# A fused attention and feed-forward layer on one core: which feed-forward weights are split when, and seven softmax steps on another engine

## The chip, the cores and the metric

The kernel runs on one core of a Trainium2 chip. A core has a matrix engine (TensorE, "PE" in the profile), a vector engine (VectorE, "DVE"), an activation engine (ScalarE, "ACT"), a general engine (GpSimd, "POOL"), and DMA queues that are fed by SyncE ("SP") and here also by ACT. Each engine runs its own instructions strictly in order and waits on semaphores for the others. The metric is the device time of one execution in microseconds; lower is better. Everything is float32; TensorE multiplies in its "fp32r" type, and the kernel gets its precision from splitting each operand into a high and a low part and adding three products.

## The reference

```python
def _A_ref(x, wqkv, wo):            # 32 heads of 16, window 8, dilation 2
    qkv = (x @ wqkv).reshape(B, S, 3, H, Dh)...
    idx = pos[:, None] - (jnp.arange(8) * 2)[None, :]
    logits = jnp.einsum("bhsd,bhswd->bhsw", q, kg) * Dh ** -0.5
    attn = softmax(where(idx >= 0, logits, -1e9), axis=-1)
    o = jnp.einsum("bhsw,bhswd->bhsd", attn, vg)
    return o... @ wo

def _B_ref(x, w1, b1, w2, b2):
    h = x @ w1 + b1
    r = where(h > 0, h, 0)
    return (r * r) @ w2 + b2

x  = A_x                            # 1 x 2048 x 512, w1 512 x 1792, w2 1792 x 512
xn = layernorm(x)
return x + _A_ref(xn, A_wqkv, A_wo) * silu(_B_ref(xn, B_w1, B_b1, B_w2, B_b2))
```

## The kernel before

**Phase 1** goes over the 2048 rows in 16 tiles of 128 (`a` and `b` are an even and an odd tile of one turn of the loop). Each tile is normalised, brought into the transposed layout and split (`xt`, high and low), and multiplied by the split weights `wq` for q, k and v: `qkv(t, s)`, twelve matmuls of 128x512 into one of four PSUM buffers. ACT copies the result to a staging tile `stg`, and per pair of tiles a DMA on SP stores it to `sq`, `sk` or `sv` in DRAM. From there the attention's loads (`load_u`, on ACT's DMA queue) bring q, k and v back in another layout.

**The attention** goes over eight units of 256 rows (u = 0 to 7) and runs on DVE beside everything else: four products and reductions for the logits (`qk`, tiles `pr` and `L`), the softmax in two parts (`soft_a`: maximum `mx`, subtraction, exponential on ACT; `soft_b`: sum `sm`, reciprocal, multiplication), four products and reductions with v (`av`, tiles `pv` and `v`), and a store to `so`. Unit 0 does its softmax in two halves; the other seven do it whole (`h is None`). The stream is written as a generator that yields an estimated cost ahead of each step, and `pump` emits steps as long as the planned clock of DVE stays near the planned clock of PE. So the numbers that are yielded set where a step stands among DVE's other instructions.

**Phase 2** goes over four chunks of 512 rows (c = 0 to 3) and, in each, over 14 slices of 128 hidden columns (f = 0 to 13): `up(c, f)` (twelve matmuls into `ph`, one of two PSUM buffers), then ACT makes relu and squares (`h`), DVE makes the low part (`lowh(f)`), and `down(c, f - 2)` (twelve matmuls into `pb`). `up(0, 0)` and `up(0, 1)` are already done at the end of phase 1. `out_product` multiplies the attention's output by `wot`; `gate` and `finish` add `b2t`, apply the gate, add the rows of x and store.

**The weights of a slice**, `w12[f]`, are 8 KB a partition: w1's columns and w2's rows, each as high and low part. `load_w` brings in both raw pieces by DMA on SP, `split_w` makes the high parts on ACT (`high`) and the low parts on GpSimd or DVE (`low`). Slices below `NKEEP` (6) live in the pool `keep` and are loaded and split in phase 1; slices 0 and 1 are loaded at the first tiles and their low parts are made on DVE. The later ones live in the pool `p2`, are loaded during chunk 0 and split three slices ahead of their use.

**The pool `p2`** is opened where phase 1's pools (`px`, `pstg`, `pwq`, `pxT`) are closed, in the same memory. The first instruction of each engine that writes into `p2` therefore waits until everything that read or wrote the closed pools is over, the last store of a staging tile among it. That is decided for the pools as a whole, not by address.

Instructions of PE, DVE, ACT and GpSimd stay in the order in which they are written; the DMAs on SP are ordered by the framework's scheduler. All compute instructions carry the line of one helper (L80) in the profile, so tiles tell them apart.

Of the kernel before, what the change touches and what calls it, by code (L numbers as in the profile page):

```python
# [8 lines left out]
F32 = mybir.dt.float32  # L9
FR = mybir.dt.float32r  # L10
# [4 lines left out]
P = 128  # L15
S = 2048
D = 512
F = 1792
KT = D // P
NF = F // P  # L20
HD = 16
W = 8
# [10 lines left out]

PASSES = ((0, 0), (0, 1), (1, 0))

NKEEP = 6

WARM = 18
WARM2 = 3
# [11 lines left out]
def body(ctx: ExitStack, tc: tile.TileContext, x, wqkv, wo, w1, b1, w2, b2, out):  # L51
# [32 lines left out]
    PE, V, A, G = Ordered(nc.tensor, "PE"), Ordered(nc.vector, "V"), Ordered(nc.scalar), Ordered(nc.gpsimd)  # L84
# [4 lines left out]
    dma = nc.sync.dma_start  # L89

    const = ctx.enter_context(tc.tile_pool(name="const", bufs=1))
# [3 lines left out]
    keep = ctx.enter_context(tc.tile_pool(name="keep", bufs=1))  # L95
# [12 lines left out]
    def piece(name):  # L108
        return keep.tile([P, 512], F32, name=name, tag="z", bufs=4)
# [76 lines left out]
                    G.memset(mask[:4 * blk + 4, :n, w], -1e9)  # L186

    b1t = const.tile([P, NF], F32, name="b1t")

    sq = dram.tile([4, S, P], F32, name="sq")  # L190
    sk = dram.tile([4, HALO + S, P], F32, name="sk")
# [32 lines left out]
    def attention():  # L224

        tiles, Ls, landing, exps = {}, {}, {}, set()

        def qk(u, s):  # L230
            i0 = 2 * s
            yield from there("k", u)
            yield from there("q", u)
            q, k, L = tiles["q", u], tiles["k", u], Ls[u]
            yield 2350
            pr = att.tile([P, W, 2 * P], F32, name=f"pr{u}_{s}", tag="pr")
            qv = q[:, i0:i0 + 2, :].rearrange("p i c -> p (i c)")[:, None, :].to_broadcast([P, W, 2 * P])
            kv = k[:, i0:i0 + 2 * W, :].rearrange("p (w i) c -> p w (i c)", i=2)
            V.tensor_mul(pr, kv, qv)
            yield 2300  # L240
            V.tensor_reduce(
                out=L[:, i0 * 8:(i0 + 2) * 8, :].rearrange("p m w -> p w m"),
                in_=pr.rearrange("p w (g d) -> p w g d", d=HD), axis=AX.X, op=OP.add)

        def there(n, u):
            while (n, u) not in tiles:
                yield None
            not_before(landing[n, u])


        def part(u, h):
            n = BI * 8 // 2
            return slice(0, 2 * n) if h is None else slice(h * n, h * n + n)

        def soft_a(u, h=None):
            yield 1500
            m = part(u, h)
            L, n = Ls[u][:, m], m.stop - m.start
            if u == 0:
                i = slice(m.start // 8, m.stop // 8)  # L260
                lm = L.rearrange("p (i h) w -> p i h w", h=8)
                V.tensor_add(lm, lm, mask[:, i, None, :].to_broadcast([P, n // 8, 8, W]))
            mx = att.tile([P, n], F32, name=f"mx{u}_{h}", tag="mx")
            V.tensor_reduce(out=mx, in_=L, axis=AX.X, op=OP.max)
            V.tensor_sub(L, L, mx[:, :, None].to_broadcast([P, n, W]))

            def exp():
                A.activation(L, L, AF.Exp)
                exps.add((u, h))

            defer(clock["V"] + BEHIND, exp)

        def soft_b(u, h=None):
            while (u, h) not in exps:
                yield None
            yield 2100
            m = part(u, h)
            L, n = Ls[u][:, m], m.stop - m.start
            sm = att.tile([P, n], F32, name=f"sm{u}_{h}", tag="sm")
            V.tensor_reduce(out=sm, in_=L, axis=AX.X, op=OP.add)  # L280
            V.reciprocal(sm, sm)
            V.tensor_mul(L, L, sm[:, :, None].to_broadcast([P, n, W]))

        def av(u, s):
            i0 = 2 * s
            yield from there("v", u)
            v, L = tiles["v", u], Ls[u]
            yield 2400

            pr = att.tile([P, W // 2, 2 * P, 2], F32, name=f"pv{u}_{s}", tag="pr")  # L290
            vv = v[:, i0:i0 + 2 * W, :].rearrange("p (a e i) (h d) -> p a e (i h) d", e=2, i=2, d=HD)
            l = L[:, i0 * 8:(i0 + 2) * 8, :].rearrange("p m (a e) -> p a e m", e=2)
            V.tensor_mul(pr.rearrange("p a (g d) e -> p a e g d", d=HD), vv,
                         l[:, :, :, :, None].to_broadcast([P, W // 2, 2, 16, HD]))
            yield 2300
            V.tensor_reduce(
                out=v[:, i0:i0 + 2, :].rearrange("p i c -> p (i c)"), in_=pr.rearrange("p w n e -> p n w e"),
                axis=AX.XY, op=OP.add)

        def store(u):  # L300
            v = tiles.pop(("v", u))
            row = so[0, u * UP:u * UP + 1, :]
            dst = bass.AP(tensor=row.tensor, offset=row.offset, ap=[[BI * P, NB], [S * P, 4], [1, BI * P]])
            dma(dst, v[:, :BI, :].rearrange("p i c -> p (i c)"))
            done_units[0] = u + 1

        def load(u, names):
            if u == NU:
                return
            for n in names:  # L310
                while done_tiles[n][0] < 2 * (u + 1):
                    yield None

                def start(n=n):
                    tiles[n, u] = load_u(n, u)
                    landing[n, u] = clock["PE"] + LOAD

                defer(max(clock["V"] + FREE if u else 0, done_tiles[n][1][u] + LAND), start)

        yield from load(0, "kqv")  # L320

        for u in range(NU + 1):
            if u < NU:
                Ls[u] = att.tile([P, BI * 8, W], F32, name=f"L{u}", tag="L", bufs=2)
                for s in range(4):
                    yield from qk(u, s)
                    if u == 0 and s % 2:
                        yield from soft_a(0, s // 2)
                if u:
                    yield from soft_a(u)  # L330
                yield from load(u + 1, "kq")
                if u == NU - 1:
                    yield from load(u, "v")
            if u == 0:
                yield from soft_b(0, 0)
            for s in range(4):
                if u > 1 or (u == 0 and s < 2) or (u == 1 and s >= 2):
                    yield from av(max(u - 1, 0), s)
            if u == 0:
                yield from soft_b(0, 1)  # L340
            if u:
                store(u - 1)
                if u < NU - 1:
                    yield from load(u, "v")
                if u < NU:
                    yield from soft_b(u)
# [17 lines left out]

    w12 = {}

    def load_w(pool, f):
        w12[f] = pool.tile([P, 2, 2, 512], FR, name=f"w{f}")

        r1, r2 = (p2.tile([P, 512], F32, name=f"{n}{f}", tag="xr", bufs=2) if f in (6, 9) else piece(f"{n}{f}")  # L370
                  for n in ("w1r", "w2r"))
        dma(r1.rearrange("p (k c) -> p k c", c=P), w1[:, f * P:(f + 1) * P].rearrange("(k p) c -> p k c", p=P))
        dma(r2, w2[f * P:(f + 1) * P, :])
        raws[f] = r1, r2

    def split_w(f, eng=G):
        for i, r in enumerate(raws.pop(f)):
            split(w12[f][:, 0, i], w12[f][:, 1, i], r, eng)

# [182 lines left out]
    norm(2)  # L562
    stats(3)
    constants()
    for f in range(2):
        load_w(keep, f)
    qkv(0, 0, lambda: highs(2, 0))
    trans(2)
    lows(2, 0)
# [10 lines left out]
    norm(4)  # L580
    norm(5)
    shuffle(4)
    split_w(0, V)
    pump(LATE)
    qkv(1, 2)
    split_w(1, V)
    pump(LATE)
    for a in range(2, NT, 2):
        b, more = a + 1, a + 2 < NT
        later = a + 4 < NT  # L590

        def weights(f):
            if 2 <= f < NKEEP:
                load_w(keep, f)
            if 2 <= f - 1 < NKEEP:
                split_w(f - 1)

        if later:
# [6 lines left out]
            mean(b + 4)  # L605
        pump(LATE)
        qkv(b, 0)
        weights(a - 5)
        if a + 2 < TURN:
            lowx(a + 2)  # L610
            trans(b + 2)
# [21 lines left out]
        if not more:  # L633
            pump()
            up(0, 1)
            lowh(0)
        weights(b - 5)
        pump(LATE)
        qkv(a, 2)
        pump(LATE)  # L640
        qkv(b, 2)
        if a == NT - 4:
            dma(b1t, b1.rearrange("(f p) -> p f", p=P))
        if a >= TPC:
            for t in (a, b):
                dma(sx[t // TPC][:, t % TPC], xt.pop(t).bitcast(F32))
# [3 lines left out]


    p2 = ctx.enter_context(tc.tile_pool(name="p2", bufs=1))
    pws, gs = {}, {}

    def down(pb, f, j):
# [60 lines left out]
        eng.tensor_add(z[:, cols], z[:, cols], xt[:, cols])  # L716
        dma(tile_rows(out, t)[:, cols], z[:, cols])

    wot = p2.tile([P, 2, 4, 512], FR, name="wot")
    b2t = p2.tile([P, D], F32, name="b2t")  # L720
    dma(b2t, b2[None, :].to_broadcast([P, D]))

    for c in range(NCH):
        last = c == NCH - 1
# [3 lines left out]
        for f in range(2, NF):  # L728
            if c == 0:
                for i in (6, 7) if f == 2 else (f + 5,):  # L730
                    if i < NF:
                        load_w(p2, i)
            up(c, f)
            pump()
            if c == 0 and f == 3:
# [4 lines left out]
                        rows = wo[q * P + 64 * i:q * P + 64 * i + 64, :].rearrange("(g p) n -> p g n", g=2)  # L740
                        dma(rwo[i][32 * q:32 * q + 32], rows)
            if c == 0:
                if NKEEP <= f + 3 < NF:
                    split_w(f + 3)
                if 6 <= f < 10:
                    split(wot[:, 0, f - 6], wot[:, 1, f - 6], rwo[(f - 6) // 2][:, (f - 6) % 2], G)
# [98 lines left out]
```

## Time and profile before

| what | us |
|---|---|
| median of 3 runs | 499.7 (496.83, 500.06, 499.7) |
| the profiled execution's own time | 495.58 |
| its span, first to last instruction | 493.8 |
| PE busy in the span | 487.5 |
| phase 1 up to the last `qkv` matmul | about 146.4 |
| chunk 0, to the start of `up(1, 2)` | about 228.5 |
| end of the last matmul | about 490.1 |

The profiled execution was 4.1 us shorter than the median of the runs, of which no trace exists. In the page's lines a group reads "line engine operation out<-in", then the count, the busy time, the mean of one, and the idle time ahead of it with what ended it. In a timeline the first two columns are the start and the duration in us. PE's busy time covers nearly the whole span; the places where something else sets the pace are short.

### The profile page before, as it was taken

The page shows a single profiled execution, that of the slowest core. Times are in us where ns is not written, and L with a number is a line of the kernel's source. Part 1 is how long each engine was busy: PE and PEld are TensorE (multiplying, and loading weights), DVE is VectorE, ACT ScalarE, POOL GpSimd, SP SyncE. Part 2 cuts the span into 40 slices and gives each one's busy share as a digit, 9 for nine tenths or more (in the row PEclk, how much of TensorE's full clock was granted, in tenths as well). Part 3 has the DMA queues.
Part 4 walks back from the last instruction along what each step waited for, and adds up shares of the span by engine and source line. Part 5 has one row for each costly group of instructions (what it writes and reads, how often), then busy time and mean ns, then how long its engine had stood idle before and what let it go on. Part 6 is the DMA issues. An engine that isn't in the chain of part 4 may idle for free.

```text
span 493.8 us, 5860 instructions
## 1 busy us (share of the span) xinstructions
PE 487.5 (99%) x2154; PEld 401.1 (81%) x2154; DVE 431.7 (87%) x370; ACT 211.0 (43%) x377; POOL 97.9 (20%) x105
## 2 busy tenths in 40 slices
PE   8999999999999999999999999999999999999997
PEld 5888888888888888887888888888888888888886
DVE  5925798998999999998999998899999889999445
ACT  5636455563343665316333324432252354313331
POOL 1311015571000779300112000112100011220000
PEclk9999999999999999999999999999999999999999
DMA  7999979769977892653406408043241805030222
GB/s 287 297 287 341 304 238 313 225 238 323 372 228 262 203 274 65 202 212 118 127 31 216 181 22 329 4 164 123 85 161 43 328 2 202 1 127 1 85 85 86
DMA packets 48520, 88.79 MB, mean 180 GB/s; under 512 B 5372, under 2 KB 32364, under 8 KB 45676
## 3 DMA queue, kind: packets, MB, share of 16 engines
q1 hardware_dynamic: 44172, 54.87, 35.3%
q10 hardware_dynamic: 4320, 33.56, 19.1%
q8 instruction: 17, 0.28, 0.2%
q14 instruction: 11, 0.09, 0.1%
HBM read 57.94 MB, written 27.32 MB: 173 GB/s over the span
## 4 chain that ended last, share of the span: by engine, by line
PE 83%; DVE 9%; issue 4%; ACT 2%; DMA 1%; ACTq 0%; POOL 0%; DVEq 0%; POOLq 0%
PE pq L80 27%; PE ph L80 24%; PE pb L80 24%; PE pw L80 8%; DVE v L80 2%; DVE pr L80 2%; DVE h L80 2%; DVE pv L80 1%; DMA x<-in_A_x 1%; ACT ph L80 0%; DVE sm_None L80 0%; ACT z L80 0%; DVE z L80 0%; ACT h L80 0%; PE pxT L80 0%
## 5 line engine op out<-in xcount | busy, mean ns | idle before, releaser
L80 PE MATMUL pb<-w,h 128*128 128x512 f32 x672 | 160.6, 389 | 0.0
L80 PEld LDWEIGHTS pb<-w,h 128*128 128x128 f32 x672 | 126.1, 188 | 26.2
L80 PE MATMUL ph<-xU,w 128*128 128x512 f32 x504 | 120.7, 389 | 0.3 <-DVE h L80 0.3
L80 PEld LDWEIGHTS ph<-xU,w 128*128 128x128 f32 x504 | 94.6, 188 | 20.2 <-DVE h L80 0.7
L80 ACT ACTIVATE ph<-ph,b1t 128x512 f32<-128x512 f32 x56 | 37.0, 661 | 163.0 <-PE ph L80 158.4
L80 PE MATMUL pq<-wq,xt 128*128 128x512 f32 x432 | 98.7, 390 | 0.0
L80 PEld LDWEIGHTS pq<-wq,xt 128*128 128x128 f32 x432 | 81.0, 188 | 17.2 <-ACT stg L80 0.3
L80 DVE TENSOR_TENSOR pr<-k,q 128x2048 f32<-128x2048 f32 x32 | 75.4, 2356 | 0.3
L80 DVE TENSOR_TENSOR pv<-v,L 128x2048 f32<-128x2048 f32 x32 | 73.8, 2305 | 0.4
L80 DVE TENSOR_REDUCE L<-pr 128x128 f32<-128x2048 f32 x32 | 72.9, 2279 | 0.6
L80 DVE TENSOR_REDUCE v<-pv 128x256 f32<-128x2048 f32 x32 | 72.9, 2279 | 0.6
L80 POOL TENSOR_TENSOR z<-z,xr 128x512 f32<-128x512 f32 x12 | 23.2, 1936 | 214.7 <-DVE z L80 209.9
L80 DVE TENSOR_TENSOR h<-ph,h 128x512 fp32r<-128x512 f32 x56 | 38.3, 683 | 19.9 <-ACT ph L80 19.9
L80 PE MATMUL pw<-wot,oT 128*128 128x512 f32 (+1 forms) x204 | 45.9, 376 | 0.0
L80 PEld LDWEIGHTS pw<-wot,oT 128*128 128x128 f32 x204 | 36.8, 188 | 7.1
L80 PE MATMUL ph<-xT,w 128*128 128x512 f32 x168 | 40.7, 391 | 0.0
L80 ACT ACTIVATE stg<-pq 128x512 f32<-128x512 f32 x48 | 27.2, 595 | 26.4 <-PE pq L80 16.9
L80 PEld LDWEIGHTS ph<-xT,w 128*128 128x128 f32 x168 | 31.5, 188 | 7.0 <-DVE h L80 0.4
L80 ACT ACTIVATE h<-ph 128x512 fp32r<-128x512 f32 x56 | 33.7, 601 | 1.8
L80 ACT ACTIVATE ph<-ph 128x512 f32<-128x512 f32 x56 | 33.3, 595 | 0.0
L80 PE MATMUL pq<-wq,xT 128*128 128x512 f32 x132 | 31.7, 398 | 0.0
L80 POOL TENSOR_TENSOR w<-w1r,w 128x512 fp32r<-128x512 f32 x12 | 18.9, 1577 | 57.1 <-DMA rwo<-in_A_wo 48.8
(66 smaller groups left out, 309.9 us busy)
## 6 DMA issues: line engine op xcount, KB each, us to landing
k<-sk ACTq DMA_DIRECT2D x8, 1408.0 KB, 8.1
v<-sv ACTq DMA_DIRECT2D x8, 1408.0 KB, 8.3
sx<-xt SPq DMA_DIRECT2D x12, 512.0 KB, 5.5
xU<-sx ACTq DMA_DIRECT2D x6, 1024.0 KB, 5.4
x<-in_A_x SPq DMA_DIRECT2D x16, 256.0 KB, 5.0
sk<-stg SPq DMA_DIRECT2D x8, 512.0 KB, 7.1
sq<-stg SPq DMA_DIRECT2D x8, 512.0 KB, 5.6
q<-sq ACTq DMA_DIRECT2D x8, 512.0 KB, 8.4
```

Source lines behind the costliest of these rows:

```text
L80: return tc.keep_in_program_order(f(*a, **k))
```

## The change

`NKEEP` goes from 6 to 3. Slices 0, 1 and 2 are loaded and split in phase 1, one per turn of the loop and later than before, all on GpSimd. Slices 3 and 4 are loaded in the turn before the last and split right after phase 1's pools are closed, into `p2`; slice 5 is loaded there, and split after `up(0, 2)`. From slice 6 on the split follows `up(0, f)` three slices ahead, as before. `b2t` moves from `p2` into the pool `const` and is loaded in phase 1. `w12[f]` is now allocated at the split and no longer at the load. In the softmax of units 1 to 7 the subtraction of the maximum and the multiplication by the reciprocal sum go from DVE to GpSimd, and the yielded costs go from 1500 to 700 and from 2100 to 1400.

```diff
-NKEEP = 6
+NKEEP = 3
...
+    b2t = const.tile([P, D], F32, name="b2t")
...
-            yield 1500
+            yield 1500 if h is not None else 700
...
-            V.tensor_sub(L, L, mx[:, :, None].to_broadcast([P, n, W]))
+            (G if h is None else V).tensor_sub(L, L, mx[:, :, None].to_broadcast([P, n, W]))
...
-            yield 2100
+            yield 2100 if h is not None else 1400
...
-            V.tensor_mul(L, L, sm[:, :, None].to_broadcast([P, n, W]))
+            (G if h is None else V).tensor_mul(L, L, sm[:, :, None].to_broadcast([P, n, W]))
...
-    def load_w(pool, f):
-        w12[f] = pool.tile([P, 2, 2, 512], FR, name=f"w{f}")
+    def load_w(f):
...
     def split_w(f, eng=G):
+        w12[f] = (keep if f < NKEEP else p2).tile([P, 2, 2, 512], FR, name=f"w{f}")
...
-    for f in range(2):
-        load_w(keep, f)
...
-    split_w(0, V)
...
-    split_w(1, V)
...
-            if 2 <= f < NKEEP:
-                load_w(keep, f)
-            if 2 <= f - 1 < NKEEP:
+            if 0 <= f < NKEEP:
+                load_w(f)
+            if 0 <= f - 1 < NKEEP:
                 split_w(f - 1)
...
-        weights(a - 5)
+        weights(a // 2 - 2)
...
-        weights(b - 5)
...
         if a == NT - 4:
             dma(b1t, b1.rearrange("(f p) -> p f", p=P))
+            dma(b2t, b2[None, :].to_broadcast([P, D]))
+            for f in (NKEEP, NKEEP + 1):
+                load_w(f)
...
     p2 = ctx.enter_context(tc.tile_pool(name="p2", bufs=1))
+    for f in (NKEEP, NKEEP + 1):
+        split_w(f)
+    load_w(NKEEP + 2)
+    wot = p2.tile([P, 2, 4, 512], FR, name="wot")
...
-                if NKEEP <= f + 3 < NF:
+                if f + 3 < NF:
                     split_w(f + 3)
```

Three places show what this does to the engines' queues. The number behind a name is the framework's; `w3`, `ph0_2`, `L2` and so on are slice 3, `up(0, 2)`, unit 2. What stands in brackets are the semaphores that an instruction waits for; DMAHW0 to 7 tell of the landing of DMAs.

ACT's queue at the end of phase 1, before: from the last copy of a `qkv` result (tile 15, v) on.

```order
L80 ACTIVATE stg14_2_1401<-pq15_2_1408 128x4x128 [waits PE_49]
L80 DMA k3_1425<-sk_141 128x1x2816 [waits DMAHW5_49,DVE_49]
L80 DMA q3_1427<-sq_140 128x1x1024 [waits DMAHW3_49,DMAHW1_49]
L80 ACTIVATE ph0_2_1454<-ph0_2_1454,b1t_139 128x512 [waits PE_49]
L80 ACTIVATE h0_2_1467<-ph0_2_1454 128x512 [waits Activation_49]
L80 ACTIVATE ph0_2_1454<-ph0_2_1454 128x512
L80 ACTIVATE L2_1245<-L2_1245 128x512 [waits DVE_49]
L80 ACTIVATE ph0_3_1493<-ph0_3_1493,b1t_139 128x512 [waits DVE_49,PE_49]
L80 ACTIVATE h0_3_1506<-ph0_3_1493 128x512 [waits Activation_49]
L80 ACTIVATE ph0_3_1493<-ph0_3_1493 128x512
L80 ACTIVATE w6_1444<-w1r6_1445 128x512 [waits DMAHW5_49,DMAHW4_49,DMAHW6_49,DMAHW2_49,DMAHW0_49]
```

The same place in the changed kernel:

```order
L80 ACTIVATE stg14_2_1387<-pq15_2_1391 128x4x128 [waits PE_49]
L80 DMA k3_1408<-sk_142 128x1x2816 [waits DVE_49]
L80 DMA q3_1410<-sq_141 128x1x1024 [waits DMAHW6_49,DMAHW0_49]
L80 ACTIVATE w3_1420<-w1r3_1254 128x512 [waits DMAHW3_49,DMAHW1_49,DMAHW7_49,DMAHW0_49,Activation_49]
L80 ACTIVATE w3_1420<-w2r3_1255 128x512
L80 ACTIVATE w4_1425<-w1r4_1258 128x512
L80 ACTIVATE w4_1425<-w2r4_1259 128x512
L80 ACTIVATE ph0_2_1447<-ph0_2_1447,b1t_139 128x512 [waits PE_49]
L80 ACTIVATE h0_2_1460<-ph0_2_1447 128x512 [waits Activation_49]
L80 ACTIVATE ph0_2_1447<-ph0_2_1447 128x512
L80 ACTIVATE L2_1203<-L2_1203 128x512 [waits Pool_49]
```

ACT's first write into `p2` was slice 6, behind the relu of `up(0, 2)` and `up(0, 3)`; it is now slice 3, ahead of both. In the changed program the DMAHW3 that it waits for is raised by the store of `stg14_2` to `sv`, the last store of phase 1.

SP's queue at that place, before:

```order
L486 DMA sk_141<-stg14_1_1330 128x4x256 [waits DMAHW6_49,Activation_49]
L486 DMA sv_142<-stg14_2_1401 128x4x256 [waits DMAHW0_49,Activation_49]
L721 DMA b2t_1438<-in_B_b2 128x512 [waits DMAHW4_49,DMAHW5_49,DMAHW1_49,DMAHW6_49,DMAHW0_49,PE_49]
L372 DMA w1r6_1445<-in_B_w1 128x4x128 [waits DMAHW2_49]
L373 DMA w2r6_1446<-in_B_w2 128x512
```

And in the changed kernel:

```order
L487 DMA sk_142<-stg14_1_1313 128x4x256 [waits DMAHW1_49,Activation_49]
L487 DMA sv_143<-stg14_2_1387 128x4x256 [waits DMAHW3_49,Activation_49]
L372 DMA w1r5_1430<-in_B_w1 128x4x128 [waits DMAHW3_49,DMAHW4_49,DMAHW2_49,DMAHW5_49,DMAHW1_49,DMAHW6_49,DMAHW0_49,DMAHW7_49,PE_49,Pool_49]
L373 DMA w2r5_1431<-in_B_w2 128x512
L741 DMA rwo0_1507<-in_A_wo 32x2x512 x2
L372 DMA w1r6_1439<-in_B_w1 128x4x128 [waits Pool_49]
```

The DMA that waits there for the same store was the one of `b2t`; it is now the load of slice 5, and the load of slice 6 behind it waits in addition until GpSimd has done slice 3.

DVE's queue near the softmax of unit 3, in chunk 0, before:

```order
L80 TENSOR_TENSOR pr3_3_1804<-k3_1425,q3_1427 128x2048 [waits DVE_49]
L80 TENSOR_REDUCE L3_1626<-pr3_3_1804 128x8x16 [waits DVE_49]
L80 TENSOR_TENSOR h0_9_1780<-ph0_9_1767,h0_9_1780 128x512 [waits PE_49,Activation_49]
L80 TENSOR_REDUCE mx3_None_1825<-L3_1626 128x64 [waits DVE_49]
L80 TENSOR_TENSOR L3_1626<-L3_1626,mx3_None_1825 128x512 [waits DVE_49]
```

And GpSimd's queue there in the changed kernel:

```order
L80 TENSOR_TENSOR w12_1782<-w1r12_1672,w12_1782 128x512 [waits DMAHW1_49,Activation_49]
L80 TENSOR_TENSOR w12_1782<-w2r12_1673,w12_1782 128x512 [waits DMAHW2_49,Activation_49]
L80 TENSOR_TENSOR wot_1434<-rwo1_1508,wot_1434 128x512 [waits Activation_49]
L80 TENSOR_TENSOR L3_1624<-L3_1624,mx3_None_1806 128x512 [waits DVE_49]
L80 TENSOR_TENSOR w13_1831<-w1r13_1721,w13_1831 128x512 [waits DMAHW3_49,Activation_49]
L80 TENSOR_TENSOR w13_1831<-w2r13_1722,w13_1831 128x512 [waits DMAHW4_49,Activation_49]
```

The subtraction for unit 3 left DVE and stands on GpSimd between the last two splits of chunk 0; ACT's exponential of that unit now waits for GpSimd.

More of the change, by code (lines that the diff above doesn't have):

```diff
@@ L365, in body @@
     w12 = {}
-    def load_w(pool, f):
-        w12[f] = pool.tile([P, 2, 2, 512], FR, name=f"w{f}")
-        r1, r2 = (p2.tile([P, 512], F32, name=f"{n}{f}", tag="xr", bufs=2) if f in (6, 9) else piece(f"{n}{f}")
+    def load_w(f):
+        r1, r2 = (p2.tile([P, 512], F32, name=f"{n}{f}", tag="xr", bufs=2) if f in (5, 8, 11) else piece(f"{n}{f}")
                   for n in ("w1r", "w2r"))
@@ L717, in finish @@
         dma(tile_rows(out, t)[:, cols], z[:, cols])
-    wot = p2.tile([P, 2, 4, 512], FR, name="wot")
-    b2t = p2.tile([P, D], F32, name="b2t")
-    dma(b2t, b2[None, :].to_broadcast([P, D]))
     for c in range(NCH):
@@ L731, in body @@
                     if i < NF:
-                        load_w(p2, i)
+                        load_w(i)
             up(c, f)
```

## The prediction

> **What bounds the kernel now.** I read the page's first line, then the chain of work that ended last in order of time, then what PE waited for.
>
> ```profile
> PE 487.5 (99%) x2154; PEld 401.1 (81%) x2154; DVE 431.7 (87%) x370; ACT 211.0 (43%) x377; POOL 97.9 (20%) x105
> ...
> 20.12 112.45 PE pq L80 x492
> ...
> 146.37 2.77 PE ph L80 x12
> 149.13 2.72 PE pb L80 x12
> 151.85 3.00 PE ph L80 x12
> ...
> 228.55 3.01 PE ph L80 x12
> 231.56 2.72 PE pb L80 x12
> ...
> 484.52 5.60 PE pw L80 x36
> ...
> PE ph L80 <- DVE h L80: 0.3, 1, 0.3
> ```
>
> PE is busy for 99% of the span. From 231.56 to the end the chain is PE alone in steps of 2.72 us for 12 matmuls, 0.227 us each. Ahead of it two steps are longer, the `up` at 151.85 (3.00) and the one at 228.55 (3.01): each 0.3 us over 2.72. In phase 1 the 492 matmuls take 112.45 where 492 x 0.227 would be 111.5: 0.9 us. So less work on DVE, at 87%, can give back 1.5 us at most (0.3 + 0.3 + 0.9); only a new wait of PE moves the time by more. The question is where the change makes PE wait.
>
> **The change at the boundary of the phases.** This is the main term. Before, around the last store of phase 1, from the timeline (start, duration) and SP's waits:
>
> ```profile
> 146.40 0.60 ACT L80 ACTIVATE stg<-pq 128x512 f32<-128x512 f32 x1 [2.12 <-PE pq L80]
> 146.47 0.52 ACTq L80 DMA_DIRECT2D k<-sk  x1
> 147.03 0.36 SPq L486 DMA_DIRECT2D sv<-stg  x1
> ...
> 151.78 3.06 PE L80 MATMUL ph<-xT,w 128*128 128x512 f32 x12
> 154.68 2.88 PE L80 MATMUL pb<-w,h 128*128 128x512 f32 x12
> 155.51 0.34 SPq L721 DMA_DIRECT2D b2t<-in_B_b  x1
> ...
> 161.53 0.63 ACT L80 ACTIVATE w<-w1r 128x512 fp32r<-128x512 f32 x1 [4.87 <-issue]
> 162.29 1.29 POOL L80 TENSOR_TENSOR w<-w1r,w 128x512 fp32r<-128x512 f32 x1 [48.79 <-DMA rwo<-in_A_wo]
> ...
> SPq L721 <- DMA sv<-stg: 7.9, 1, 7.9
> ...
> DMA to landing us min/median/max: 3.2/6.8/10.4
> ```
>
> The store of the last v tile is issued at 147.03, and the first DMA into `p2` (`b2t`) gets free at 155.51, waiting for that store. So the closed pools are free at 155.5. Before, nobody on PE's path cared: `up(0, 3)`, which starts at 151.78, read a slice split long ago. Now slice 3 is itself the first tile in `p2`, and ACT's copy of its high part waits for the same store.
>
> The sum: free at 155.5; ACT's first copy 0.63, to 156.15; GpSimd's low part begins 0.13 later (162.29 against 161.53 + 0.63) and takes 1.29, to 157.6. The first two matmuls of `up(0, 3)` need the high part, the third the low part. Before, the third began ten matmuls ahead of the next group, at 154.68 - 10 x 0.227 = 152.4. It now begins at 157.6: **5.2 us** of wait. Its bounds come from the last row, the landing times of all staging stores: landing 3.2 us after the issue ends (147.39) gives 150.6 and w3's low part at 152.7, 0.3 us of wait; 10.4 gives 157.8 and 7.5 us. I take the store's own 8.1, since the order of ACT's and SP's queues there is the same: the 1.4 MB load of k is issued just ahead of the store, with which it shares the DMA engines.
>
> Behind ACT's waiting copy stand three more copies, relu and squares of `up(0, 2)`, the exponential of unit 2, slice 5's copies and the relu of `up(0, 3)`.
>
> ```profile
> 164.90 0.61 ACT L80 ACTIVATE w<-w1r 128x512 fp32r<-128x512 f32 x1
> 165.41 0.62 ACT L80 ACTIVATE w<-w2r 128x512 fp32r<-128x512 f32 x1
> 165.93 0.65 ACT L80 ACTIVATE ph<-ph,b1t 128x512 f32<-128x512 f32 x1
> 166.61 0.60 ACT L80 ACTIVATE h<-ph 128x512 fp32r<-128x512 f32 x1
> 166.91 0.68 DVE L80 TENSOR_TENSOR h<-ph,h 128x512 fp32r<-128x512 f32 x1
> 167.11 0.59 ACT L80 ACTIVATE ph<-ph 128x512 f32<-128x512 f32 x1
> ```
>
> Copies follow each other in 0.52, so the relu begins at 155.5 + 4 x 0.52 = 157.6 and the last square ends 1.8 later (165.93 to 167.70), at 159.4; `lowh(2)` takes 0.68, to 160.1, while DVE idles for some 4 us. That one frees the buffer for `up(0, 4)`, which follows ten matmuls (2.3) and a `down` (2.7) behind 157.6, at 162.6: 2.5 us to spare, nothing. On SP the load of slice 5 waits where `b2t` waited, with `wo`'s pieces and slice 6 behind it: slice 5 is needed two groups after `up(0, 4)`, at 168; the load of slice 6 that was issued in this place had its first piece copied at 161.53, so nothing. Slice 4's parts are ready by 157.6 + 3 x 1.29 = 161.5: nothing.
>
> **The clock.** A stop of this length may cost more than itself.
>
> ```profile
> 491.00:492.00 1.00, 0.00 (x0) 0.00 (x0) 0.03 (x1) 0.00 (x0) 0.00 (x0) 1.00 0.10 33
> 492.00:493.00 1.00, 0.00 (x0) 0.00 (x0) 0.00 (x0) 0.00 (x0) 0.00 (x0) 0.60 0.30 100
> ...
> 1.34 3.51 PE L80 MATMUL warm<-ident 128*128 128x128 f32 x18 [1.34 <-POOL mhalf L80]
> ...
> 2.60:3.60 1.00, 1.00 (x7) 1.00 0.94 305
> 4.10:4.60 0.50, 0.50 (x7) 1.00 0.78 291
> ```
>
> PE's last matmul ends at 490.1 (484.52 + 5.60 in the chain). The granted clock is still 1.00 in the microsecond from 491 and averages 0.60 in the next: at half speed for 0.8 of it, so it fell at about 492.2, 2.1 us after PE's last work. At the start the warming transposes begin at 1.34; 7 of them stand in a microsecond, and from 4.1 on as many in half of one: 2.8 us of work until the pace doubled. In the changed kernel PE has nothing from 151.85 (149.13 + 2.72) to 156.15, 4.3 us, which is twice the 2.1. I expect the clock to fall there, and the first 2.8 us of matmuls after 157.6 to run at half pace: **1.4 us** more. Bounds: 0 (it doesn't fall) and 2.8 (it stays down for twice as long).
>
> [...]
>
> **The softmax on GpSimd and the splits.** Groups with their mean in ns, and one place where both engines met:
>
> ```profile
> L80 DVE TENSOR_TENSOR L<-L,mx_None 128x512 f32<-128x512 f32 x7 | 5.7, 812 | 0.2
> L80 DVE TENSOR_TENSOR L<-L,sm_None 128x512 f32<-128x512 f32 x7 | 5.6, 800 | 0.2
> L80 POOL TENSOR_TENSOR w<-w1r,w 128x512 fp32r<-128x512 f32 x12 | 18.9, 1577 | 57.1 <-DMA rwo<-in_A_wo 48.8 <-ACT w L80 8.3
> L80 POOL TENSOR_TENSOR wot<-rwo,wot 128x512 fp32r<-128x512 f32 x4 | 11.9, 2980 | 0.0
> L80 DVE TENSOR_TENSOR w<-w1r,w 128x512 fp32r<-128x512 f32 x2 | 1.4, 690 | 0.7 <-ACT w L80 0.7
> L80 DVE TENSOR_TENSOR pr<-k,q 128x2048 f32<-128x2048 f32 x32 | 75.4, 2356 | 0.3
> ...
> 94.89 3.24 DVE L80 TENSOR_TENSOR pr<-k,q 128x2048 f32<-128x2048 f32 x1
> 95.94 3.35 POOL L80 TENSOR_TENSOR w<-w2r,w 128x512 fp32r<-128x512 f32 x1
> ```
>
> DVE loses 5.7 + 5.6 us of softmax and four low parts of 0.69, some 14 us in all. GpSimd gains 14 operations; it showed none of this kind, so I bound one by 1.29 (a low part alone) and 2.98 (the `wot` group), and take 1.6, its low parts' mean: 22 us on an engine at 20%. None of DVE's relief is worth more than the waits of PE that it ends: I take **0.3 us**, the wait at 228.55. The other, at 151.85, goes under in the new one; phase 1's 0.9 us is no recorded wait, and I give it nothing. On ACT the exponential now waits for GpSimd; the one that matters is unit 3's, behind slice 12 and the last part of `wot`. GpSimd's order there is fixed by ACT's copies, which come with PE, so it too stands 6 us later and adds one operation of 1.3 to 3.0; the cover is the buffer that lets PE run two `up` ahead, and if it were gone the price would be those 3.0.
>
> The price of sharing shows in the last two rows: a product on DVE that starts during GpSimd's work takes 3.24 against a mean of 2.36, and a low part on GpSimd that starts during DVE's takes 3.35 against the 1.29 above. So part of DVE's relief is taken back; PE doesn't notice, in either direction. [...]
>
> In phase 1 the loads of slices 0 and 1 go from the first tiles to later, and it loads five slices where it loaded eight (0 to 5, 7 and 8, by SP's queue), 1.5 MB less; b2t's 256 KB join. PE shows no wait for a DMA there, so nothing.
>
> **The sum.** 5.2 + 1.4 - 0.3 = +6.3 us. On the profiled execution's 495.58 that is 501.9; on the median of the runs, 499.7, it is **506.0 us**, and that is my forecast, since the changed kernel will be timed as those runs were. The profiled execution stands 4.1 below the median, and what the 4.1 are no trace tells.
>
> **The rivals.** A measurement of this kernel can tell about 1%, 5 us, from no change.
>
> *Not slower: the store lands early.* If the load of k were issued after the store, or the DMA engines were emptier, the store could land 3.2 us after its issue, as the fastest did: 0.3 us of wait, no stop long enough for the clock, 499.7 + 0.3 - 0.3 = 499.7. With the clock's 1.4 the change is 1% slower when the store lands after 154.2 and within 1% before. Against it: k's load stands ahead of the store in the order, and what it waits for on DVE comes earlier than before. 8 in 100.
>
> *The clock holds.* [...] Against it: 4.3 us of stop against 2.1. 13 in 100.
>
> *Phase 1 holds the 4.1 us.* ACT sat 8 us ahead of its copies at 133.66, behind a DMA issue that waited for a store:
>
> ```profile
> 133.66 2.07 ACT L80 ACTIVATE stg<-pq 128x512 f32<-128x512 f32 x4 [8.18 <-DVE L L80]
> ```
>
> Four copies came at once then, as many as `qkv` has buffers. If the runs of 499.7 lose their 4.1 us there, fewer loads and an earlier end of unit 0 may free it: 506.0 - 4.1 = 501.9. 10 in 100.
>
> *GpSimd comes late.* If unit 3's exponential or slice 13 holds up ACT or PE, 3 us more: 509. 12 in 100.
>
> *The change doesn't do what it says.* DVE may get no relief, since a product that meets GpSimd's step loses 3.24 - 2.36 = 0.9, more than the 0.8 that left; then the 0.3 is missing: 506.3, inside my forecast.
>
> **How the numbers follow.** My forecast, 504.5 to 507.5, has 54 in 100; 3 are left for a gain that I don't see. Slower by over 1% (above 504.7): most of the forecast (50), GpSimd late (12), a third of the held clock (4): 0.66. Faster by over 1% (below 494.7): 0.03. Within: 0.31. The range goes from 500.5 (it leaves out the early store) to 509.0 (half of GpSimd late).
>
> **What would show it.** In the changed profile: a wait of PE of 4 to 6 us near 152, its `up` released by GpSimd or ACT on `w`, ACT idle until about 8 us after the store's issue; a granted clock of 0.5 for some 3 us behind it; `up` and `down` back to 2.72 from there; no wait near 228; `L<-L,mx` and `L<-L,sm` on POOL. I am wrong if PE runs through at 152, or if the chain shows GpSimd in chunks 1 to 3.

## The result, and the profile after

The changed kernel takes 506.3 us (median of four runs, 505.43 to 508.13), the kernel before 499.8 in the same comparison (four runs, 496.83 to 500.06). The ratio is 1.0156, with an interval of 1.0113 to 1.0199: slower by more than 1%. The forecast was 506.0.

The page of the changed kernel has PE a little longer busy in a longer span, less work on DVE and more on GpSimd:

```profile
span 503.0 us, 5875 instructions
...
PE 490.7 (98%) x2154; PEld 402.2 (80%) x2154; DVE 422.4 (84%) x352; ACT 210.8 (42%) x377; POOL 130.2 (26%) x123
```

The chain of the changed kernel around the boundary of the phases (start, duration, what) leaves PE for the first time since 97 us:

```profile
143.98 5.50 PE pq L80 x24
149.48 0.02 issue
149.50 0.61 ACT stg L80
150.11 0.02 issue
150.13 8.60 DMA sv<-stg
...
158.90 0.64 ACT w L80
...
159.66 1.29 POOL w L80
160.96 0.04 issue
161.00 3.60 PE ph L80 x10
164.60 2.74 PE pb L80 x12
167.34 2.72 PE ph L80 x12
```

This is the stop that was forecast, link by link: the last copy out of PSUM, the store of the last v tile (8.2 us from the end of its issue at 150.49 to its landing at 158.72), ACT's copy into the first tile of `p2`, GpSimd's low part, and the third matmul of `up(0, 3)`. From there the chain is PE alone. PE's steps are 2.72 us again from 167.34 on.

PE's waits in the changed kernel (us in total, times, longest):

```profile
PE ph L80 <- ACT w L80: 4.7, 1, 4.7
PE pq L80 <- ACT stg L80: 1.6, 2, 1.0
```

The second row was not forecast. It lies in phase 1, at 92 and 96 us. The PE records of the two traces can be cut in three pieces: to the 61st matmul, where full groups begin (16.50 before, 16.74 after); from there to the first `up` (115.91 before, 118.76 after); and the rest to the last matmul (357.42 before, 363.55 after). Of the 9.2 us between the two traces, 6.1 are in the last piece, 2.9 in phase 1, 0.2 at the start.

### The profile page after: what moved, and what is told of

The parts are those of the page before. It is cut to its first block, busy times and chain, and to the rows that moved or that the text cites. A ratio compares the mean times of both kernels' runs of the same rounds, so it can differ in the third digit from the quotient of the medians.

```text
span 503.0 us, 5875 instructions
## 1 busy us (share of the span) xinstructions
PE 490.7 (98%) x2154; PEld 402.2 (80%) x2154; DVE 422.4 (84%) x352; ACT 210.8 (42%) x377; POOL 130.2 (26%) x123
## 4 chain that ended last, share of the span: by engine, by line
PE 79%; DMA 9%; DVE 6%; ACT 2%; issue 2%; SPq 1%; POOL 1%; DVEq 0%; ACTq 0%; POOLq 0%
PE ph L80 30%; PE pb L80 30%; PE pq L80 10%; PE pw L80 9%; DMA xb<-xn 5%; DMA x<-in_A_x 2%; DMA sv<-stg 2%; DVE L L80 2%; SPq L445 1%; DVE pr L80 1%; DVE pxT L80 1%; POOL rs L80 1%; DVE wq L80 1%; DVE xt L80 1%; ACT xn L80 0%
## 5 line engine op out<-in xcount | busy, mean ns | idle before, releaser
L80 PE MATMUL pq<-wq,xt 128*128 128x512 f32 x432 | 99.8, 391 | 1.7 <-ACT stg L80 1.6
L80 DVE TENSOR_TENSOR pr<-k,q 128x2048 f32<-128x2048 f32 x32 | 78.8, 2461 | 0.3
L80 PE MATMUL ph<-xT,w 128*128 128x512 f32 x168 | 42.2, 400 | 5.0 <-ACT w L80 4.7
L80 POOL TENSOR_TENSOR z<-z,xr 128x512 f32<-128x512 f32 x12 | 25.5, 2127 | 67.1 <-DVE z L80 57.7
L80 POOL TENSOR_TENSOR L<-L,mx_None 128x512 f32<-128x512 f32 x7 | 15.5, 2218 | 92.2 <-DVE mx_None L80 92.2
```

What stands on the lines that cost most here:

```text
L80: return tc.keep_in_program_order(f(*a, **k))
```

## The experiments

Three things were to be told apart: whether the stop at the boundary is the wait for the closed pools, and why the store is slow; what the clock takes; and where phase 1's 2.9 us come from. Each ratio is to the kernel before, run in the same comparison.

### The two slices out of the new pool

```diff
-        w12[f] = (keep if f < NKEEP else p2).tile(...)
+        w12[f] = (keep if f < NKEEP + 2 else p2).tile(...)
```

> The changed kernel, but the tiles of slices 3 and 4 come from the pool `keep`, as before the change; their splits stay where the change put them. Theory (PE's stop at the boundary is the wait for the closed pools, and the half clock is its consequence): ACT's copy of slice 3 follows its last copy out of PSUM within a microsecond, PE has no wait near 155, the granted clock stays 1.00 there, and the time falls by 5.5 + 1.1 us, to 499.7, with phase 1 still some 3 us longer than in the kernel before. Rival 1 (the late split itself stops PE, whatever the pool): PE still waits 3 us or more for slice 3, and the time is above 503. Rival 2 (the stop moves to slice 5, whose raw pieces still lie in the new pool): PE waits near 165 instead, 502 to 504.

Measured: 499.5 us, ratio 1.0018 (0.9988 to 1.0048). ACT in this kernel:

```profile
150.39 0.60 ACT L80 ACTIVATE stg<-pq 128x512 f32<-128x512 f32 x1 [2.12 <-PE pq L80]
...
151.62 0.63 ACT L80 ACTIVATE w<-w1r 128x512 fp32r<-128x512 f32 x1 [0.63 <-DVE h L80]
...
155.40 0.62 ACT L80 ACTIVATE L<-L 128x512 f32<-128x512 f32 x1
163.58 0.63 ACT L80 ACTIVATE w<-w1r 128x512 fp32r<-128x512 f32 x1 [7.56 <-DMA rwo<-in_A_wo]
```

The copy of slice 3 follows 0.6 us behind the last copy out of PSUM, where it waited 8.8. PE runs through, and the granted clock stays 1.00. With the place of the splits unchanged, the pool alone makes the difference: the theory holds, rival 1 falls. Rival 2 is half right: ACT now waits 7.6 us at slice 5, whose raw pieces are loaded into `p2` behind the last store (the row names a DMA of `wo`, the last of that wait by the profile), its relu of `up(0, 3)` stands behind that, and PE loses 1.2 us at 167.7, and 1.0 at 234. No loss against the kernel before can be measured any more.

### The store ahead of unit 3's loads

The planner starts the loads of k and q of unit 3 later, by 9 us of its clock:

```diff
-                defer(max(clock["V"] + FREE if u else 0, done_tiles[n][1][u] + LAND), start)
+                defer(max(...) + (9000 if u == 3 and n != "v" else 0), start)
```

> The changed kernel with the loads of k and q of unit 3 issued 9 us later by the planner, so that 1.9 MB no longer stand ahead of the last v store. Theory (the store lands 8.2 us after its issue because it shares the DMA engines with those loads): it lands 3 to 5 us after its issue, PE's stop at the boundary falls from 5.5 us to 0.3 to 2.5, the clock may not fall, and the time is 500.5 to 503.5. Rival (the store is slow by itself): it still lands 7 us or more after its issue, and the time is 505 to 507. A second risk: DVE waits for the later k, and PE for DVE, which gives part back.

Measured: 501.6 us, ratio 1.0063 (1.0033 to 1.0093). The timeline of this kernel:

```profile
151.64 0.36 SPq L487 DMA_DIRECT2D sv<-stg  x1
...
154.85 0.64 ACT L80 ACTIVATE w<-w1r 128x512 fp32r<-128x512 f32 x1 [3.24 <-DMA sv<-stg]
...
157.61 2.57 PE L80 MATMUL ph<-xT,w 128*128 128x512 f32 x10 [0.69 <-POOL w L80]
```

Without 1.9 MB ahead of it, the store is over within 2.8 us of the end of its issue (ACT goes on at 154.85), where ACT went on 8.4 us after it in the changed kernel. PE loses 0.9 us in place of 5.5, and the clock stays up. So the store is not slow by itself, and the rival "the store lands early" was a real point of decision that only the order of three DMAs kept from coming true. Some of the gain goes again: PE loses 1.4 us at 174 and 235 together, where DVE comes later.

### Work for PE in the stop

Transposes of the identity, whose result nobody uses, ahead of `up(0, 3)`: 60 in `warm_stop`, 42 in `warm_stop2`. In the second the planner isn't told of them.

```diff
+                if f == 3:
+                    hold = psT("hold")
+                    for n in range(42):
+                        tc.keep_in_program_order(nc.tensor.transpose(hold[:, :P], ident, ident))
             up(c, f)
```

> The changed kernel, with 60 transposes of the identity (result unused, 0.071 us each at full clock, 4.3 us) on PE ahead of `up(0, 3)`, that is inside its stop. Theory (the half clock after the stop costs what it shows, 1.1 us in the profiled run of the changed kernel, up to 2 in others): the granted clock stays 1.00 through 165, PE resumes at the same place, and the time falls by 1.1 to 2, to 504.3 to 505.2. Rival 1 (transposes don't hold the clock): 506. Rival 2 (they outlast the stop or hold something up): 506.5 or more.

Measured: 511.9 us, ratio 1.0268 (1.0253 to 1.0284). The clock did stay up at the first stop, but a second one came:

```profile
169.35 2.88 PE L80 MATMUL pb<-w,h 128*128 128x512 f32 x12
176.75 3.78 PE L80 MATMUL ph<-xT,w 128*128 128x512 f32 x8 [4.51 <-DVE h L80]
```

The planner had counted the 60 transposes as 9 us of PE (150 ns each in its table) and put that much more attention work on DVE ahead of `lowh(3)`, which ended at 176.7. So the run says nothing on what the half clock costs. It shows that what the planner believes is part of a change, and was the reason for the next run.

> As warm_stop, but with 42 transposes (0.107 us each in warm_stop's trace, 4.5 us) and without telling the planner of them, so that DVE's order is that of the changed kernel. Theory (the half clock costs PE 1.1 to 2 us after the stop): the granted clock stays 1.00 at the boundary, no second stop follows, and the time is 504.3 to 505.2 where the changed kernel had 506.3. Rival (the clock's part is nothing, or warm_stop's second stop came from the transposes and not from the planner): 506 or more.

Measured: 503.2 us, ratio 1.0096 (1.0068 to 1.0125), 3 us under the changed kernel by the medians, with intervals that overlap. The ten matmuls behind the stop show the clock's own part. First the changed kernel, then `warm_stop2`, then three kernels (below) that have the stop as well, `weights_only`, `b2t_p2` and `b2t_slot`:

```profile
161.00 3.60 PE L80 MATMUL ph<-xT,w 128*128 128x512 f32 x10 [0.34 <-POOL w L80]
```

```profile
161.69 2.55 PE L80 MATMUL ph<-xT,w 128*128 128x512 f32 x10 [0.66 <-POOL w L80]
```

```profile
160.69 3.99 PE L80 MATMUL ph<-xT,w 128*128 128x512 f32 x10 [0.17 <-POOL w L80]
```

```profile
157.62 4.16 PE L80 MATMUL ph<-xT,w 128*128 128x512 f32 x10 [0.17 <-POOL w L80]
```

```profile
161.31 4.63 PE L80 MATMUL ph<-xT,w 128*128 128x512 f32 x10 [0.17 <-POOL w L80]
```

Ten matmuls take 2.55 at full clock and 3.60, 3.99, 4.16 and 4.63 without: the half clock costs 1.05, 1.44, 1.61 and 2.08 us. The first two matmuls run slower too, but the third waits for GpSimd anyway. By the traces the theory holds. The profiled run of the changed kernel is a cheap case: its mean granted clock was 0.997, that of its other three runs 0.992 to 0.993, as in the traces of the three kernels with the dearer stops (0.992). That may be a part of why the median fell by 3 us and not by 1 to 1.5; the rest lies within the intervals and isn't explained.

The clock in the changed kernel, microsecond by microsecond (busy share of PE, PEld, DVE, ACT, POOL with counts, granted clock, DMA share, GB/s):

```profile
159.00:160.00 1.00, 0.37 (x1) 0.32 (x2) 0.00 (x0) 1.00 (x3) 0.34 (x1) 0.91 0.00 0
160.00:161.00 1.00, 0.66 (x2) 0.00 (x1) 0.00 (x0) 1.00 (x3) 1.00 (x2) 0.50 0.61 169
...
162.00:163.00 1.00, 1.00 (x4) 0.78 (x3) 0.21 (x1) 1.00 (x3) 1.00 (x2) 0.50 1.00 258
163.00:164.00 1.00, 1.00 (x6) 0.79 (x5) 1.00 (x2) 1.00 (x3) 1.00 (x2) 0.88 1.12 188
```

### The two halves of the change alone

`soft_only` is the kernel before with the four lines of the softmax; `weights_only` is the changed kernel without them.

> The kernel before with the softmax part of the change alone (the subtraction and the scaling of seven units on GpSimd, with the changed planner's figures). Theory: DVE loses some 11 us of work and gets part of it back in longer products; PE is bound by its own work, so 499.7, less 0 to 0.5. Rival 1: DVE's relief ends waits that the records don't show, 497 or less. Rival 2: GpSimd comes late, at an exponential or at a slice, 502 or more.

Measured: 497.6 us, ratio 0.9971 (0.9945 to 0.9998). PE's waits in it, which all lie in the first 23 us:

```profile
PE warm L80 <- POOL mhalf L80: 1.3, 1, 1.3
PE pxT L80 <- DVE xn L80: 0.3, 1, 0.3
```

From the first `up` on it takes 356.6 us where the kernel before takes 357.4: the longer steps at 151.85 and 228.55 are gone. That is 0.8, a little more than the 0.5 that I expected at most. PE never waits for the softmax on GpSimd. This half of the change is a small gain, just clear of the noise, and the fastest kernel of the study.

> The changed kernel with the subtraction and scaling back on DVE, with the planner's figures of before: the part of the change that concerns weights, alone. Theory: both the stop at the boundary and phase 1's loss belong to the weights and b2t, 506.3 plus 0 to 0.5. Rival (the softmax on GpSimd, or its place in the planner's order, makes phase 1 longer): phase 1 ends 2 to 3 us earlier, 503 to 504.

Measured: 504.8 us, ratio 1.0105 (1.0064 to 1.0146). The stop is there (PE waits 4.9 us for ACT), and phase 1 takes 118.2, 0.6 less than in the changed kernel and not the 2 to 3 of the rival. So the stop and the longer phase 1 belong to the weights, not to the softmax. The time itself lies between the two forecasts, 1.5 us under the changed kernel by the medians, with intervals that overlap. The two halves don't add up: 0.9971 times 1.0105 is 1.0076, and the change has 1.0156 with 1.0113 as its lower bound. The traces don't show this difference (spans of 503.1 us here and 503.0 with the softmax on GpSimd), and no run explains it.

### Phase 1

SP's queue at the start, first of the kernel before, then of the changed one (start, issue time):

```profile
12.55 0.80 SPq L373 DMA_DIRECT2D w2r<-in_B_w  x1
13.85 0.38 SPq L643 DMA_DIRECT2D b1t<-in_B_b  x1
15.24 3.56 SPq L486 DMA_DIRECT2D sk<-stg  x1
```

```profile
12.82 0.76 SPq L373 DMA_DIRECT2D w2r<-in_B_w  x1
14.11 0.38 SPq L639 DMA_DIRECT2D b1t<-in_B_b  x1
15.46 3.54 SPq L640 DMA_DIRECT2D b2t<-in_B_b  x1
19.09 0.57 SPq L487 DMA_DIRECT2D sk<-stg  x1
```

Two things stand here that I had missed. The loads of slices 0 and 1 did not leave the start: their last piece is issued at 12.82 (before 12.55), because the scheduler, not the written order, places SP's DMAs. And b2t's load, written near the end of phase 1, came to the start too, ahead of the first k store. My theory was that this pushes the stores, with them the loads of unit 0 and the shuffles `xb`, and that PE meets the lag at 92. Four kernels test it: b2t back in `p2`; a load of 7 KB in its place; such a load, of 128 KB, in the kernel before; and SP's DMAs in written order.

```diff
-            dma(b2t, b2[None, :].to_broadcast([P, D]))
+            dma(tiny, b1.rearrange("(f p) -> p f", p=P))            # b2t_slot
...
+            dma(more, b2[None, :D // 2].to_broadcast([P, D // 2]))  # before_more
...
-    dma = nc.sync.dma_start
+    dma = Ordered(nc.sync).dma_start                             # sp_order
```

> The changed kernel, but b2t lies in `p2` and is loaded there, as before the change, so it leaves the start of SP's queue. Theory (phase 1's 3.1 us begin with b2t's load at 15.46, which pushes the stores behind it by one DMA and makes the first v store wait for the load of k, 35.0 where it was issued at 28.3): the first pair of DVE transposes out of xb comes at 37.6 instead of 38.65, the third near 68 instead of 71.4, PE's waits at 92 and 96 are gone or halved, and the time falls by 1.5 to 3.1 us, to 503.2 to 504.8; the stop at the boundary stays. Rival (the lag comes from GpSimd's splits beside DVE's products, or from chance in the landings): waits at 92 and 96 stay, 506.

> The changed kernel with b2t back in `p2`, but with another, small load (7 KB, a second copy of b1, which nothing reads) in the place that b2t's load had at the start of SP's queue. It tells whether b2t's load cost phase 1 its 3 us by its place or by its data. Theory 1 (place: one more DMA in the queue ahead of the first k store moves each later one by a turn, and the stores meet other loads): the first matmul of a full pair to the first `up` takes 118 to 119 us as in the changed kernel, the first transposes out of xb come at 38.6, and the time is 505 to 506. Theory 2 (data: 256 KB written as 128 rows while the first stores wait): phase 1 is as with b2t gone, 115.7 us, first transposes near 36.5, and the time 503 to 504.

> The kernel before, with one more load (half of b2 to all partitions, 128 KB, which nothing reads) where the change put b2t's load. If such a load ahead of the first k store is what makes phase 1 longer, whatever else changed, phase 1 is 1.5 to 3 us longer than the 115.9 us of the kernel before, and the time is 500.5 to 502. Rival (it costs only together with the other loads of the change): 115.9 us, 499.

> The changed kernel with SP's DMAs held in the order in which the code is written, so that b1t, b2t and slices 0 and 1 are really loaded late: the first k store is SP's 16th DMA where it was the 21st. Theory (phase 1 is long when the first transposes out of xb come more than 21 us after the first full pair of matmuls, and that is set by how early SP gets to the first stores): the first transposes come at 36.5 or earlier, phase 1 takes 115.7 us as with b2t gone, and with the stop at the boundary left as it is the time is 502.5 to 504. Rival 1 (only one DMA more or less matters, not their number): as b2t_p2, 503.8. Rival 2 (written order holds SP up elsewhere, where a DMA that isn't ready blocks the next): 506 or more.

From the PE and DVE records of every trace, the start of the first transpose out of `xb`, counted from the 61st matmul; phase 1, from there to the first `up`; from the first `up` to the last matmul; and the median with its ratio.

```
kernel        first transpose  phase 1  rest    median  ratio
soft_only           19.1        115.7   356.6   497.6   0.9971 (0.9945 to 0.9998)
b2t_p2              20.0        115.7   364.0   503.8   1.011  (1.0049 to 1.0171)
before              20.9        115.9   357.4
before_more         21.0        117.5   357.9   499.2   1.0014 (0.9989 to 1.0038)
keep5_lag           21.6        118.9   358.1   499.0   1.0017 (0.9994 to 1.0039)
after               21.9        118.8   363.6   506.3   1.0156 (1.0113 to 1.0199)
b2t_slot            22.1        119.3   364.6   505.3   1.0142 (1.0122 to 1.0162)
keep5               22.1        119.8   359.0   499.5   1.0018 (0.9988 to 1.0048)
weights_only        22.2        118.2   364.2   504.8   1.0105 (1.0064 to 1.0146)
warm_stop           22.4        118.8   370.3   511.9   1.0268 (1.0253 to 1.0284)
late_k3             22.7        120.2   359.3   501.6   1.0063 (1.0033 to 1.0093)
warm_stop2          22.8        119.5   362.6   503.2   1.0096 (1.0068 to 1.0125)
in written order:
sp_order            19.2        117.2   367.6   507.4   1.0186 (1.0156 to 1.0216)
keep5_sp            19.4        117.1   361.8   500.9   1.0055 (1.0037 to 1.0073)
```

With SP in its scheduled order, phase 1 is short where the first transpose comes within 20.9 us and 1.6 to 4.3 us longer where it comes later. The way from there to PE stands in the changed kernel's chain: the shuffle that lands at 89.80, ACT's normalisation of the tile behind it, GpSimd's power for its variance, and ACT's copies out of PSUM, which stand behind that in ACT's queue.

```profile
80.77 9.03 DMA xb<-xn
...
91.18 0.80 ACT xn L80
...
93.05 2.58 POOL rs L80
...
96.64 0.59 ACT stg L80
97.23 0.04 issue
97.27 38.39 PE pq L80 x168
```

But what makes the first transpose late is not settled. With b2t gone it came early and phase 1 was as before (`b2t_p2`), as the theory has it; a load of 7 KB in its place costs as much as b2t (`b2t_slot`), so it would be the turn in the queue and not the data. Against it: `keep5_lag` (below) has the same start of SP's queue as `b2t_p2` and yet a late first transpose and 118.9 us; and the extra load in the kernel before costs nothing by the median. One trace of each kernel is too little to tell, when the runs of the kernel before alone spread from 496.5 to 503.0 us. In written order (`sp_order`) the first transpose is early and phase 1 yet 1.3 us longer, with a wait at 95 that remains. The boundary gets worse: two stores of `xt` now stand behind the last v store, and PE waits 7.6 us for ACT's copy. Rival 2 of that run holds, and my theory falls in its simple form.

### A version with both repairs

`keep5_lag`: slices 3 and 4 in `keep`, b2t as before, and each split of chunk 0 one group later; `keep5_sp`: the same with SP in written order.

```diff
-                if f + 3 < NF:
-                    split_w(f + 3)
+                if 5 <= f + 2 < NF:
+                    split_w(f + 2)
```

> The changed kernel with slices 3 and 4 in `keep`, b2t in `p2` as before the change, and the splits of phase 2 one group later (after `up(c, f)` that of slice f + 2), so that ACT doesn't wait for slice 5 ahead of a relu. Theory (boundary 6.6, phase 1 3 and slice 5's wait 1.2 us were the whole loss): no wait of PE over 0.5 us after its 60th matmul, 496.5 to 498.5, at or below the kernel before. Rival (a group later is too late for a slice): waits of PE for GpSimd on w, above 499.

> keep5_lag with SP's DMAs in written order as well. Theory: as keep5_lag, with more room in phase 1: 496 to 498, the lowest of all if the start of SP's queue was the last thing that held PE. Rival: SP blocks at a DMA that isn't ready, as in sp_order's rival 2, 499 or more.

Measured: 499.0 us, ratio 1.0017 (0.9994 to 1.0039), and 500.9, ratio 1.0055 (1.0037 to 1.0073). `keep5_lag` has no wait of PE in phase 2 that the list of waits records, but phase 1's copies still hold PE for 1.7 us in its trace, and it is no faster than the kernel before, above the 496.5 to 498.5 that I expected. In `keep5_sp` slice 5 comes late (PE waits 2.4 us for GpSimd on `w`). So of all versions only `soft_only` is below the kernel before, by 0.3%.

## Why the prediction was right, step by step

- **The boundary, 5.2 us.** Right, in mechanism and size. The third matmul of `up(0, 3)` came at 161.00; without the stop it would have come at 155.5 (152.4 and the 3.1 by which phase 1 ended later), so 5.5. The store took 8.2 where 8.1 was taken, and ACT began 0.2 after the landing. One reading was off: the landing times that gave the bounds count from the start of an issue (the changed kernel's store has 8.60 in the chain), not from its end, so both bounds of the wait stood 0.4 us too high; the 5.2 does not rest on them. `keep5` shows that the pool is the cause, `late_k3` that the store is slow because of the loads ahead of it.
- **The clock, 1.4 us.** It fell, and it cost what was forecast or somewhat less or more: 1.05 in the trace of the changed kernel, 1.44, 1.61 and 2.08 in the three others with the same stop. But the working was a misreading, so the nearness is in part luck. There is no fixed delay of 2.1 us after PE's last work: here the clock fell 4.9 us after it, at 159.8, just as PE had resumed, and the half speed lasted 3.41 us by the trace's record of the clock; in `b2t_p2` it fell 2.5 us after it and lasted 6.8 (154.24 to 161.08, from the granted clock of each microsecond). A stop shorter than the 4.3 us seems to be enough: in `keep5_sp`, where PE's wait was 2.4 us, the mean granted clock of the profiled run was 0.995, and in `keep5_lag`, without such a wait, 1.000. The costs lie on both sides of 1.4, since a part of the slow time fell on matmuls that waited anyway (here 1.2 of the 3.41, ahead of 161.00), and since the slow time could last twice as long.
- **DVE's relief, 0.3 us.** Too small by a little. PE's wait near 228 is gone. In the kernel before, the two groups of matmuls from 225.40 to 231.40 took 6.00 us where two of 2.72 take 5.44, so it was worth 0.6. `soft_only` gained 0.8 after phase 1, this and the 0.3 at 151.85. DVE's busy time fell by 9.3 of the 14 us that left it; a part came back as longer products, as forecast:

```profile
L80 DVE TENSOR_TENSOR pr<-k,q 128x2048 f32<-128x2048 f32 x32 | 78.8, 2461 | 0.3
...
L80 POOL TENSOR_TENSOR L<-L,mx_None 128x512 f32<-128x512 f32 x7 | 15.5, 2218 | 92.2 <-DVE mx_None L80 92.2
```

- **The softmax on GpSimd, nothing.** Right. The fourteen operations took 23.1 us where 22 were estimated, 2.22 in the mean for the subtraction, 1.09 for the scaling. PE waits for none of them; ACT waits 1.0 us for them, in two exponentials together.
- **What stands behind ACT's wait, slice 4, and the loads of slices 5 and 6, nothing.** Right: after the third matmul of `up(0, 3)` PE has no wait in chunk 0.
- **Phase 1's loads, nothing.** This step failed in its premise, and against the trace in its size. I had the loads of slices 0 and 1 leave the first tiles; they stayed, and b2t's load came there as well. That PE showed no wait for a DMA did not mean that it had room: the shuffles reach it through ACT's queue. Against the trace of before, 2.9 us are missing here. Against the medians they are not: with the stop taken away (`keep5`) the ratio is 1.0018, though its trace has one of the longest phases 1 in the table.
- **Which time to add to.** The choice of the median was what made the forecast right; from the profiled 495.58 it would have been 501.9. That it came within 0.3 us is in part luck: the four runs of the kernel before in this comparison had a median of 499.8, those of the larger samples (15 to 19 runs) 498.1 to 498.8. By the ratio of 1.0156 the change costs 7.8 us, 5.6 to 9.9 by its interval, where 6.3 were forecast. In the comparisons of this study the kernel before had medians of 498.1 to 499.8, and its runs went from 496.5 to 503.0; the profiled execution lies below all of them. Its phase 1 is at the short end of a table that reaches from 115.7 to 120.2. That the missing 4 us lie there is likely from this, but no trace of a slower run of that kernel shows it.
- **The rivals.** The store that lands early is what `late_k3` made true. The clock held nowhere with the full stop, except where PE was given work. "Phase 1 holds the 4.1 us" was right on the place, as far as the last point goes, and wrong in that the change would free them. GpSimd was not late, and DVE got relief.

## What to carry to other kernels

A tile from a pool that reuses the memory of closed pools made its first writer wait here until the last store out of them had landed (ACT 8.8 us, against 0.6 in `keep5`); put the first tiles that the bounding engine needs into memory that was free all along, and order that last DMA ahead of bulk loads (PE's 5.5 us fell to 0.9 in `late_k3`). A profile taken on the fast edge of a kernel's spread makes a comparison of two traces show losses that the medians don't have: take away one cause and time it before a second difference between traces is believed. Where a scheduler places the DMAs, read its order, not the code's.

## What the hardware showed that was not expected

- The granted clock's half-speed stretch at the boundary lasted 3.41 us in the changed kernel and 6.8 in `b2t_p2`, two steps of 3.41. The stop's length alone doesn't set it: PE's wait was 4.7 us in the first and 4.5 in the second. The mean granted clock of the profiled runs goes with that: 0.997 in the changed kernel, 0.992 with waits of 4.5 to 4.9 us in `b2t_p2`, `weights_only` and `b2t_slot`, 0.989 with 7.6 in `sp_order`, 0.995 with 2.4 in `keep5_sp`; with 0.7 in `late_k3` it was 0.998, as in the kernel before, where the clock fell only behind PE's last work. The time from the clock's rise near the start to its fall is a whole number of these steps too (6.23 to 159.83 in the changed kernel, 45 of them; 4.10 to 492.20 in the kernel before, 143). From this it seems that what a stop costs beyond itself, 1.05 to 2.08 us here, depends on where it falls among the steps.
- In scheduled order the 20th DMA that SP issued took 3.49 to 3.62 us to issue in eleven of twelve traces, whether it was the k store (3.56 and 3.49), b2t's load (3.54) or a load of 7 KB (3.62); in `soft_only` it took 2.41. What stands behind it waits. In written order, where the k store was the 15th DMA, neither it (0.38) nor the 20th (0.39) took that long. What is waited for there, no run shows.
- Two fp32 operations of the same shape, 128x512 with a broadcast operand, differed on GpSimd by what DVE did beside them. The subtraction took 3.06 to 3.07 us in the four units where a product `pv` on DVE had begun 0.16 to 0.17 us before it, and 1.09 in the three where none had. The multiplication, which never met such a start, took 1.09 each time. On DVE they had taken 0.81 and 0.80.
